# Top-k attention with a feed-forward block on one Trainium2 core: the turned weights go from SBUF to SBUF in 16 transfers, and small operations and the centring go to ScalarE

## The chip, the core and the metric

The kernel runs on one core of a Trainium2 chip. The metric is the device time of one execution in microseconds (us). Before the change it is 1734.24 us, the median of three runs (1732.39 to 1737.46). The kernel is written in Bass with the Tile layer, which places semaphores and buffers; the order of the instructions on each engine is the order in which the Python code emits them.

## The reference, cut to what matters

```python
# q, k, v: (8, 8, 576, 64) float32; top_k = 32
scores = q @ k.T / sqrt(64)
kth    = the 32nd largest score of each row
scores = where(scores >= kth, scores, -1e9)
attn   = softmax(scores)                  # per row, eps 1e-9 in the denominator
x      = (attn @ v) with heads joined     # (8, 576, 512)
mu, var = mean and variance of x's rows
xn     = (x - mu) / sqrt(var + 1e-6) * g_ln
out    = x + relu(xn @ w_ch1) @ w_ch2     # 512 -> 2048 -> 512
```

So there are 64 heads of 576 queries, each with a selection of 32 of 576 scores per row, and after them a feed-forward block over 4608 rows of 512.

## The kernel before, in words

**Units.** The queries of a pair of heads are cut into five units: four of 128 queries (with both heads side by side, tiles of 128x2x576) and a rest of 64 queries (both heads stacked in one tile of 128x576). There are 160 units in all, 20 for each of the 8 elements of the batch. Units are grouped into jobs (`Job`, `Group`): for the later batch elements four triples (two whole units and the rest unit, one triple for each pair of heads) and then four pairs (two whole units). A group ends in one product with v.

**Steps.** The main loop (from L1183) runs one step for each unit, and in a step it emits the work of several units at different ages. Step n does, in this order on each engine:

- PE: the scores of unit n+1 (L390), then, when a group is due, its product with v (`values`, L611 and L618), then the feed-forward matmuls (L756, L913) that `fill` hands out in small shares, and the turning back of a group's result (`place`, L653).
- ScalarE (ACT): copies of the new scores from PSUM to a tile `sc` (L371), the exponentials of unit n-2 (`weigh`, L496), the mask of unit n-1 (`mask`, L483), and evacuations for the feed-forward part.
- VectorE (DVE): for unit n the halving (L411, L412) and the four rounds of finding the top values (`select`, L433, L419, L425); `watch` (L452), which notes whether the selection may have been short; and `move(ex)` (L524) for unit n-2, in the middle of the step, ahead of the third round `select(u, 2)`.
- GpSimd (POOL): `lower` of unit n-1 (L488), sums for the feed-forward part, `prepare(u)` (L446: minus the row's largest score, as the exponential's bias) at the end of the step, and the centring of x in `Block.stats` (L687, L690).

**Turned weights.** The product with v needs the weights with the keys on the partitions. 118 of the 160 units (`u.moved`) are turned this way: DVE transposes 32x32 blocks of `e` into the unit's score tile `sc` (L524). Then the blocks have to change partitions. `send` (L540) stores the whole tile, 128 rows of 4608 bytes, to a DRAM tile `turned`, and `bring` (L532) loads it back into `pt` in four transfers of 32x4 rows of 1152 bytes. The tile `pt` has one buffer, so the first `bring` of a group waits until the product of the group before has read it. The score tiles `sc` have five buffers; one is free again when its `send` has landed. The other units are turned by PE.

**Queues.** All transfers but eight loads at the start are issued by SyncE (SP), in the order of the code: the heads of the next job (`load`, L293, eight for each fresh pair of heads), values (`load_values`, L305 and L309, four for each job), heads kept in DRAM for the second job of a pair of heads and fetched again (L334, L341), denominators of rest units (L601), prepared weights of the feed-forward block (L983), and stores of the result (L730). What should be issued later than it is known lies in a list `Later` and comes due after so many calls of `fill` (ticks): a `send` after 2 ticks, its `bring` 4 ticks later, a load of heads after 4. As the program is built, eight semaphores serve SP's transfers in turn, and each transfer waits for the one eight places before it.

**Feed-forward work.** When the rows of a block of 256 are complete, the block's matmuls go into a list with a cost each, and `slot(n)` spreads what is listed evenly over the steps up to the next block, or to the end (`END`). They fill PE beside the attention; what is left after the last unit runs alone at the end. A block is given a number of steps after its last unit, by `step` at L1053.

Of the kernel before, what the change touches and what calls it, by code (L numbers as in the profile page):

```python
# [9 lines left out]
AF = mybir.ActivationFunctionType  # L10
ALU = mybir.AluOpType
FP32 = mybir.dt.float32
# [7 lines left out]
STEEP = 2.0**90  # L20
# [9 lines left out]
def compute(  # L30
# [12 lines left out]
    nc = tc.nc  # L43
    P = nc.NUM_PARTITIONS
    B, H, S, D = q.shape
# [6 lines left out]
    scale = 1.0 / float(D) ** 0.5  # L52
# [4 lines left out]
    def pool(name, bufs, **kw):  # L57
        return ctx.enter_context(tc.tile_pool(name=name, bufs=bufs, **kw))
# [3 lines left out]
    HALF = S // 2  # L62
# [13 lines left out]
    brief_small = pool("brief_small", 2)  # L76
# [6 lines left out]
    xtpool = pool("xt", 1)  # L83
    hpool = pool("h", NF // 2)
    turnedpool = pool("turned_kq", 2, space=bass.MemoryType.DRAM)
    hbmpool = pool("hbm", 4, space=bass.MemoryType.DRAM)
    formpool = pool("forms", 1, space=bass.MemoryType.DRAM)
    psps = pool("ps", 5, space=PSUM)
    mmps = pool("mmps", 3, space=PSUM)
# [1 line left out]
    def const(shape, name):  # L91
        return consts.tile(shape, FP32, tag=name, name=name)
# [15 lines left out]
    if doubt is not None:  # L108
        watched = const([P, 34], "watched")
# [76 lines left out]
    now = [-1]  # L186
# [36 lines left out]
    todo = []  # L223
# [6 lines left out]
    def pop():  # L230
        kind, cost, run, may = todo.pop(0)
        assert not may or may()
        owed[0] -= cost
        run()
# [23 lines left out]
                run()  # L258

    sums_later, ends_later, stores = Later(), Later(), Later()  # L260
    sends, brings, loads = Later(), Later(), Later()

    def fill(least=0):
        tick[0] += 1
        ends_later.settle(END_AGE)
        loads.settle(LOAD_AGE)
        brings.settle(BRING_AGE)
        sends.settle(SEND_AGE)
        fetch_forms(FETCH_AGE)
        owed[0] = min(owed[0] + share[0], 6.0)  # L270
        while todo and (not todo[0][3] or todo[0][3]()):
            if owed[0] < todo[0][1] / 2 and least <= 0:
                break
            least -= 1
            pop()
# [162 lines left out]
            u.top = m  # L438
        u.thr = m

    def prepare(u):

        nt = len(u.tiles)
        u.bias, u.edge = u.thr[:, 0:nt, 5], u.thr[:, 0:nt, 6]
        eng = nc.vector if u.i < CONVERTING else nc.gpsimd
        eng.tensor_scalar(u.bias, u.top[:, 0:nt, 0], -scale, 0.0, ALU.mult, ALU.add)  # L446

    def watch(u):

        nt = len(u.tiles)  # L450
        c = 1 + 2 * (u.i % 16)
        nc.vector.tensor_tensor(  # L452
            watched[:, c : c + nt], u.hi[:, 0:nt, HALF + 7], u.thr[:, 0:nt, 7], ALU.subtract
        )
        if u.i % 16 == 15 or u.i == N - 1:
            u.ends_watch = True

    def settle_watch():

        for out, first, op in ((0, 0, ALU.max), (33, 1, ALU.min)):  # L460
            nc.vector.tensor_reduce(
                watched[:, out : out + 1], watched[:, first : first + 33],
                mybir.AxisListType.X, op,
            )
# [13 lines left out]
    def mask(u, t):  # L478
        if u.e is None:
            u.e = epool.tile([P, 2, S], FP32, tag="e", name="e")  # L480
        if t == 0:
            nc.scalar.mul(u.edge, u.thr[:, 0 : len(u.tiles), 7], STEEP)
        nc.scalar.activation(  # L483
            u.e[:, t], u.sc[:, t], AF.Relu, bias=u.edge[:, t : t + 1], scale=-STEEP
        )

    def lower(u, t):
        nc.gpsimd.tensor_tensor(u.e[:, t], u.e[:, t], u.sc[:, t], ALU.subtract)  # L488
# [30 lines left out]
    def move(u):  # L519

        i0 = place_of(u)
        ni, nb = P // 32, (2 * J + 1) * 32
        blocks = u.sc[:].rearrange("p t n -> p (t n)")
        nc.vector.transpose(  # L524
            blocks.rearrange("p (j c n) -> p j c n", j=ni, n=32),
            u.e[:].rearrange("p t n -> p (t n)").rearrange("p (c j k) -> p j c k", j=ni, k=32),
        )
        hbm = hbmpool.tile([P, 2 * S], FP32, tag="turned", name="turned")

        def bring():  # L530
            for j in range(ni):
                nc.sync.dma_start(  # L532
                    u.group.pt[j * 32 : (j + 1) * 32, i0 : i0 + ni].rearrange(
                        "k i c n -> k i (c n)"
                    ),
                    hbm[:, j * nb : (j + 1) * nb].rearrange("(i k) x -> k i x", k=32),
                )

        def send():
            nc.sync.dma_start(hbm[:], blocks)  # L540
            brings.add(bring)

        sends.add(send)

# [120 lines left out]
    class Block:  # L665
# [9 lines left out]
        def stats(self, i):  # L675
            x = self.x[i]
            if self.mv is None:
                self.mv = small.tile([P, J, 2], FP32, tag="mv", name="mv")
                self.rstd = small.tile([P, J], FP32, tag="rstd", name="rstd")
            st = brief_small.tile([P, 6], FP32, tag="st", name="st")  # L680
            nc.vector.bn_stats(out=st[:], in_=x)
            nc.vector.bn_aggr(out=self.mv[:, i, :], in_=st[:])
            if now[0] <= gives_first:
                nc.vector.tensor_scalar_sub(x, x, self.mv[:, i, 0:1])
            else:
                less = brief_small.tile([P, 1], FP32, tag="less", name="less")
                nc.gpsimd.tensor_scalar(  # L687
                    less[:], self.mv[:, i, 0:1], -1.0, 0.0, ALU.mult, ALU.add
                )
                nc.gpsimd.tensor_scalar(x, x, 1.0, less[:], ALU.mult, ALU.add)  # L690
            self.step[i] = now[0]

        def centred(self, i):
# [246 lines left out]

    PER_ROW = 1.71e-3
    SUM_AGE, END_AGE, FETCH_AGE, STORE_AGE = 7, 6, 10, 8
    SEND_AGE, BRING_AGE, LOAD_AGE = 2, 4, 4
    blocks = []
    plain_done, formed, used, fetched = [None], [None], [], [0]

# [41 lines left out]
    def fetch_forms(age):  # L988
        if done(formed[0]):
            free = 4 + sum(tick[0] - x >= age for x in used)  # L990
            while fetched[0] < min(free, 8 * (len(blocks) - 1)):
                fetch_form()
# [19 lines left out]
    units = []  # L1012
# [5 lines left out]
            g.last = len(units) - 1  # L1018
        j.last = len(units) - 1
    N = len(units)  # L1020
    END = N + 7

    fresh = []
    for j in jobs:
# [7 lines left out]
    CONVERTING = max(n for n in batches if batches[n]) + 2  # L1032
    EARLY = jobs[NHP].first
# [16 lines left out]
    for j in jobs:  # L1050
        if j.hp == NHP - 1:
            b = j.b
            step = j.last + (3 if j.last < EARLY else 4 + units[j.last].moved)  # L1053
            tiles = [(b, qt) for g in j.groups for qt in g.qts if qt < J]
            dsts = [[(out[b, t[1] * P : (t[1] + 1) * P, :], full)] for t in tiles]
            if jobs.index(j) == NHP - 1:
                step -= 1
                j.groups[0].quick = True
            if tiles:
                add_block(step, tiles, dsts)  # L1060
            if J in j.groups[0].qts and b % 4 == 3:
# [17 lines left out]
    def at(i):  # L1079
        return units[i] if 0 <= i < N else None  # L1080
# [64 lines left out]
    def slot(n):  # L1145
# [5 lines left out]
        if n > last_give:  # L1151
            even = left / max(1, END - 1 - n)
        else:
# [28 lines left out]
    weights(-1, 1)  # L1182
    for n in range(END):  # L1183
        now[0] = n
# [7 lines left out]
        u, nxt, mk = at(n), at(n + 1), at(n - 1)  # L1192
        ex, g = after(n)
# [3 lines left out]
        moved = ex is not None and ex.moved  # L1197
# [9 lines left out]
        if u:  # L1207
            halve(u)
            select(u, 0)
        if doubt is not None and mk:  # L1210
            watch(mk)
        for j in fetches.get(n, []):
            fetch_heads(j)
        stores.settle(STORE_AGE)
# [30 lines left out]
        sums_later.settle(SUM_AGE)  # L1245
        for den in recips.pop(n, []):
            nc.vector.reciprocal(den, den)
        if doubt is not None and at(n - 1) and at(n - 1).ends_watch:
            settle_watch()
            if n == N:  # L1250
                tell()
        if n in turns:
            turn_heads(turns[n])
# [6 lines left out]
        if mk and not early:  # L1260
            mask(mk, 0)
# [9 lines left out]
            lower(mk, 0)  # L1271
        if len(parts) > 2:
            parts[1]()
        if moved:
            move(ex)
        if u:
            select(u, 2)
        for blk, i in rows_of.pop(n, []):
# [27 lines left out]
            weights(n, 1)  # L1306
        if u:
            select(u, 3)
            prepare(u)
        for x in (g, quick):  # L1310
            if x and x.job.hp == NHP - 1:
                for qt in x.qts:
# [10 lines left out]
                for x in (r - 1, r):  # L1323
                    arrived(n, ("r", x), rs[x])
        fill()
    while todo or any(x.waiting for x in (sums_later, ends_later, stores, sends, brings)):
        tick[0] += 1
        stores.settle(2)
        brings.settle(1)
        sends.settle(1)  # L1330
        ends_later.settle(1)
        sums_later.settle(1)
        fetch_forms(1)
        if todo:
            pop()
# [50 lines left out]
```

## Time and profile before

| | |
|---|---|
| median of three runs | 1734.24 us (1732.39 to 1737.46) |
| profiled execution: its own time, its span | 1737.59 us, 1735.7 us |
| busy: PE, DVE, ACT, POOL | 1485.2, 1467.9, 1032.2, 1051.8 us |
| granted TensorE clock, mean | 0.932 |
| transfers issued by SP, their issue time added up | 1527, 750 us |
| time that packets took, share of 16 DMA engines | 55.8% |
| from the start of unit 20 to the last watch of unit 159 (7 batch elements) | 1364.1 us |
| span after the last watch (1609.7 us), mostly feed-forward work on PE | 126 us |

How to read it. The profile is of one execution, 3.4 us above the median; sums against the trace are made with its span. "Busy" is the time in which an engine ran an instruction; the waits, by engine and by line, are in a view of their own, as are the waits of SP's queue. SP is not counted among the busy engines, since it only issues; but an issue has a duration too, and the timeline of SP shows it: the second column of a row is the time that SP spent on the issues of that row, which is not the time of the transfer. The time from issue to landing is given apart, in the table of transfers.

### The profile page before, as it was taken

What the parts mean: (1) busy time and instruction counts of PE and PEld (TensorE: products, weight loads), DVE (VectorE), ACT (ScalarE), POOL (GpSimd) and SP (SyncE); (2) the same over time, 40 slices, a digit from 0 to 9 for tenths busy, and PEclk for the clock granted to TensorE, in tenths of its full rate; (3) what the DMA queues carried; (4) which work ended last, traced back from release to release, by engine and by line L of the source; (5) the groups of instructions that cost most, each with busy time, mean ns of one, the idle gap of its engine ahead of it and who ended that gap; (6) DMA issues with size and microseconds to landing.
All of it is one profiled execution on the core that took longest, in us unless ns stands there. A gap on an engine that the chain in (4) does not pass through costs nothing.

```text
span 1735.7 us, 26165 instructions
## 1 busy us (share of the span) xinstructions
PE 1485.2 (86%) x7412; PEld 1110.8 (64%) x7412; DVE 1467.9 (85%) x4090; ACT 1032.2 (59%) x2662; POOL 1051.8 (61%) x1321
## 2 busy tenths in 40 slices
PE   2558887887788888788899989999899899989997
PEld 1336455655566665566677766776677676768886
DVE  6979999989898998889998998899989998984100
ACT  6777765755566564556566756676566665644411
POOL 4668868646556564556656766576656665746334
PEclk9768898988999898899999999999999999989999
DMA  7525657744565465545775586556755676453411
GB/s 190 134 66 181 200 123 216 226 140 136 151 182 151 145 187 154 152 144 153 212 181 159 161 221 161 175 167 181 199 172 150 168 214 181 139 141 110 124 45 51
DMA packets 392068, 275.19 MB, mean 159 GB/s; under 512 B 254436, under 2 KB 358376, under 8 KB 391912
## 3 DMA queue, kind: packets, MB, share of 16 engines
q1 hardware_dynamic: 387176, 272.81, 55.8%
q8 instruction: 62, 1.02, 0.3%
q10 hardware_dynamic: 4736, 0.59, 0.2%
q14 instruction: 94, 0.77, 0.1%
HBM read 177.47 MB, written 95.81 MB: 157 GB/s over the span
## 4 chain that ended last, share of the span: by engine, by line
PE 41%; DVE 30%; ACT 8%; DMA 8%; POOL 7%; SPq 3%; issue 2%; DVEq 0%; ACTq 0%; POOLq 0%
PE ops L913 14%; PE hps L756 12%; DVE m L433 9%; DVE hi L419 7%; PE av L611 6%; DVE sc L524 5%; PE scps L390 4%; DMA pt<-turned 3%; POOL e L488 3%; DVE lo L412 3%; ACT e L496 2%; DVE hi L411 2%; DVE hi L425 2%; PE av L618 2%; SPq L532 2%
## 5 line engine op out<-in xcount | busy, mean ns | idle before, releaser
L488 POOL TENSOR_TENSOR e<-e,sc 128x576 f32<-128x576 f32 x288 | 424.0, 1482 | 295.8 <-ACT e L483 292.5
L756 PE MATMUL hps<-xT,w 128*128 128x256 f32 x2304 | 533.4, 384 | 3.2 <-ACT xT L718 3.2
L756 PEld LDWEIGHTS hps<-xT,w 128*128 128x128 f32 x2304 | 432.1, 192 | 74.3 <-issue 12.3
L433 DVE MAX8 m<-hi 128x8 f32<-128x296 f32 (+1 forms) x1152 | 469.9, 442 | 1.1
L419 DVE MATCH_REPLACE8 hi<-m,hi 128x288 f32<-128x288 f32 (+1 forms) x864 | 377.1, 441 | 0.0
L913 PE MATMUL ops<-w,h 128*128 128x256 f32 x1360 | 321.3, 385 | 0.0
L371 ACT COPY sc<-scps 128x288 f32<-128x288 f32 x576 | 202.7, 406 | 190.1 <-PE scps L390 167.2
L913 PEld LDWEIGHTS ops<-w,h 128*128 128x128 f32 x1360 | 256.2, 193 | 42.1 <-issue 7.5
L611 PE MATMUL av<-pt,vb 128*64 128x256 f32 (+2 forms) x1088 | 175.6, 473 | 101.4 <-DMA pt<-turned 62.7
L496 ACT ACTIVATE e<-e,m 128x576 f32<-128x576 f32 x288 | 224.9, 787 | 60.2 <-POOL e L488 59.9
L524 DVE STREAM_TRANSPOSE sc<-e 128x1152 f32<-128x1152 f32 x118 | 160.2, 1358 | 109.5 <-ACT e L496 103.0
L483 ACT ACTIVATE e<-sc,m 128x576 f32<-128x576 f32 x288 | 217.5, 774 | 5.2
L611 PEld LDWEIGHTS av<-pt,vb 128*64 128x64 f32 x1088 | 91.3, 161 | 174.4 <-issue 94.9
L446 POOL TENSOR_SCALAR m<-m 128x2 f32<-128x2 f32 (+1 forms) x143 | 109.3, 764 | 135.1 <-DVE m L433 132.0
L779 ACT ACTIVATE h<-hps 128x512 f32<-128x512 f32 x144 | 85.4, 594 | 102.3 <-PE hps L756 101.9
L412 DVE TENSOR_TENSOR lo<-sc 128x576 f32<-128x576 f32 (+1 forms) x160 | 144.2, 901 | 0.0
L390 PE MATMUL scps<-kT,qT 64*128 64x288 f32 x512 | 96.8, 480 | 46.0 <-DVE qT L320 40.6
L411 DVE TENSOR_TENSOR hi<-sc 128x576 f32<-128x576 f32 (+1 forms) x160 | 124.9, 780 | 6.6 <-ACT sc L371 6.4
L913 PE MATMUL ops<-wt,s 128*128 128x256 f32 x544 | 128.0, 383 | 0.0
L390 PE MATMUL scps<-kT,late_qT 64*128 64x288 f32 (+3 forms) x832 | 122.2, 412 | 2.1 <-ACT pt L565 2.1
L425 DVE MAX8 hi<-lo 128x8 f32<-128x288 f32 x288 | 117.8, 443 | 0.0
L913 PEld LDWEIGHTS ops<-wt,s 128*128 128x128 f32 x544 | 102.0, 192 | 16.6 <-issue 2.1
(104 smaller groups left out, 1664.4 us busy)
## 6 DMA issues: line engine op xcount, KB each, us to landing
turned<-sc SPq DMA_DIRECT2D x118, 576.0 KB, 3.3
pt<-turned SPq DMA_DIRECT2D x472, 144.0 KB, 3.0
w<-forms SPq DMA_DIRECT2D x136, 256.0 KB, 4.1
vb<-in_v_dram SPq DMA_DIRECT2D x136, 128.0 KB, 3.3
raw<-in_moe_w_ch_dram SPq DMA_DIRECT2D x32, 512.0 KB, 4.5
kT<-kept SPq DMA_DIRECT2D x36, 288.0 KB, 3.4
kin<-in_k_dram SPq DMA_DIRECT2D x128, 72.0 KB, 2.4
kept<-kT SPq DMA_DIRECT2D x32, 288.0 KB, 2.6
```

The source lines that it names most:

```text
L371: nc.scalar.copy(u.sc[:, t, s * HALF : (s + 1) * HALF], made[s][t][:, 0:HALF])
L390: nc.tensor.matmul(ps[i * R : i * R + ql, o : o + width], qT[r, q0 : q0 + ql], kT[r, k0 : k0 + width], start=True, stop=True,)
L412: nc.vector.tensor_tensor(lo, a, b, ALU.min)
L419: nc.vector.match_replace(x, m[:, t, :], x, LOWEST)
L433: nc.vector.max(m[:, t, :], u.hi[:, t, 0:width])
L483: nc.scalar.activation(u.e[:, t], u.sc[:, t], AF.Relu, bias=u.edge[:, t : t + 1], scale=-STEEP)
L488: nc.gpsimd.tensor_tensor(u.e[:, t], u.e[:, t], u.sc[:, t], ALU.subtract)
L496: nc.scalar.activation(u.e[:, t], u.e[:, t], AF.Exp, bias=u.bias[:, t : t + 1], scale=-scale, accum_out=g.den[:, col : col + 1],)
L524: nc.vector.transpose(blocks.rearrange("p (j c n) -> p j c n", j=ni, n=32), u.e[:].rearrange("p t n -> p (t n)").rearrange("p (c j k) -> p ...
L611: nc.tensor.matmul(av[h * D : (h + 1) * D, 0 : g.nq], vb[:, h * J + c, :], g.pt[:, 0 : g.nq // 32, 5 * h + c, :], start=(c == 0), stop=False,)
L756: nc.tensor.matmul(ps[0][:, side * N : (side + 1) * N], w1[:, c, f * P : (f + 1) * P], self.xT[:, c, 0:N], start=(c == 0), stop=(c == NC - 1),
L913: nc.tensor.matmul(bank[name][:, 0:Q], a(j), rhs, start=first and j == 0, stop=(j == G - 1), skip_group_check=not first,)
```

## The change

1. `send` and `bring` are one: the DRAM tile `turned` is gone, and `send` issues 16 transfers from SBUF to SBUF, each of 32 rows of 288 elements (1152 bytes), 36 KB, from 32 partitions of `sc` to 32 partitions of `pt`.
2. `move(ex)` is emitted at the end of the step, after `select(u, 3)`, and no longer ahead of `select(u, 2)`.
3. `prepare` (POOL, in the first steps DVE) and `watch` (DVE) are gone; `mask` does the same on ACT: the scaled maximum by one `mul`, the watched difference by one activation for each tile.
4. The centring in `Block.stats` goes from POOL to ACT and becomes due two ticks later (`CENTRE_AGE`).
5. A block whose last unit is moved is given one step later, `settle_watch` and `tell` come one step later, and the loop has one more step (`END = N + 8`).

```diff
-    sends, brings, loads = Later(), Later(), Later()
+    sends, loads, centres = Later(), Later(), Later()
...
-        brings.settle(BRING_AGE)
+        centres.settle(CENTRE_AGE)
...
-    def prepare(u):
-        nt = len(u.tiles)
-        u.bias, u.edge = u.thr[:, 0:nt, 5], u.thr[:, 0:nt, 6]
-        eng = nc.vector if u.i < CONVERTING else nc.gpsimd
-        eng.tensor_scalar(u.bias, u.top[:, 0:nt, 0], -scale, 0.0, ALU.mult, ALU.add)
-
-    def watch(u):
-        nt = len(u.tiles)
-        c = 1 + 2 * (u.i % 16)
-        nc.vector.tensor_tensor(
-            watched[:, c : c + nt], u.hi[:, 0:nt, HALF + 7], u.thr[:, 0:nt, 7], ALU.subtract
-        )
...
     def mask(u, t):
...
         nc.scalar.activation(
             u.e[:, t], u.sc[:, t], AF.Relu, bias=u.edge[:, t : t + 1], scale=-STEEP
         )
+        if t == 0:
+            nc.scalar.mul(u.bias, u.top[:, 0:nt, 0], -scale)
+        if doubt is not None:
+            c = 1 + 2 * (u.i % 16) + t
+            nc.scalar.activation(
+                watched[:, c : c + 1], u.thr[:, t, 7:8], AF.Identity,
+                bias=u.hi[:, t, HALF + 7 : HALF + 8], scale=-1.0,
+            )
...
-        hbm = hbmpool.tile([P, 2 * S], FP32, tag="turned", name="turned")
-        def bring():
-            for j in range(ni):
-                nc.sync.dma_start(
-                    u.group.pt[j * 32 : (j + 1) * 32, i0 : i0 + ni].rearrange(
-                        "k i c n -> k i (c n)"
-                    ),
-                    hbm[:, j * nb : (j + 1) * nb].rearrange("(i k) x -> k i x", k=32),
-                )
         def send():
-            nc.sync.dma_start(hbm[:], blocks)
-            brings.add(bring)
+            for i in range(ni):
+                for j in range(ni):
+                    nc.sync.dma_start(
+                        u.group.pt[j * 32 : (j + 1) * 32, i0 + i].rearrange("k c n -> k (c n)"),
+                        blocks[i * 32 : (i + 1) * 32, j * nb : (j + 1) * nb],
+                    )
...
-                nc.gpsimd.tensor_scalar(
-                    less[:], self.mv[:, i, 0:1], -1.0, 0.0, ALU.mult, ALU.add
-                )
-                nc.gpsimd.tensor_scalar(x, x, 1.0, less[:], ALU.mult, ALU.add)
+                def centre():
+                    less = brief_small.tile([P, 1], FP32, tag="less", name="less")
+                    nc.scalar.mul(less[:], self.mv[:, i, 0:1], -1.0)
+                    nc.scalar.activation(x, x, AF.Identity, bias=less[:])
+                    self.step[i] = now[0]
+                centres.add(centre)
+                return
...
-    END = N + 7
+    END = N + 8
...
-            step = j.last + (3 if j.last < EARLY else 4 + units[j.last].moved)
+            step = j.last + (3 if j.last < EARLY else 4 + 2 * units[j.last].moved)
...
-        if moved:
-            move(ex)
         if u:
             select(u, 2)
...
         if u:
             select(u, 3)
-            prepare(u)
+        if moved:
+            move(ex)
```

More of the change, by code (lines that the diff above doesn't have):

```diff
@@ L85, in compute @@
     turnedpool = pool("turned_kq", 2, space=bass.MemoryType.DRAM)
-    hbmpool = pool("hbm", 4, space=bass.MemoryType.DRAM)
     formpool = pool("forms", 1, space=bass.MemoryType.DRAM)
@@ L439, in select @@
         u.thr = m
-    def prepare(u):
-        nt = len(u.tiles)
-        u.bias, u.edge = u.thr[:, 0:nt, 5], u.thr[:, 0:nt, 6]
-        eng = nc.vector if u.i < CONVERTING else nc.gpsimd
-        eng.tensor_scalar(u.bias, u.top[:, 0:nt, 0], -scale, 0.0, ALU.mult, ALU.add)
-    def watch(u):
-        nt = len(u.tiles)
-        c = 1 + 2 * (u.i % 16)
-        nc.vector.tensor_tensor(
-            watched[:, c : c + nt], u.hi[:, 0:nt, HALF + 7], u.thr[:, 0:nt, 7], ALU.subtract
-        )
-        if u.i % 16 == 15 or u.i == N - 1:
-            u.ends_watch = True
     def settle_watch():
@@ L480, in mask @@
             u.e = epool.tile([P, 2, S], FP32, tag="e", name="e")
+        nt = len(u.tiles)
         if t == 0:
-            nc.scalar.mul(u.edge, u.thr[:, 0 : len(u.tiles), 7], STEEP)
+            u.bias, u.edge = u.thr[:, 0:nt, 5], u.thr[:, 0:nt, 6]
+            nc.scalar.mul(u.edge, u.thr[:, 0:nt, 7], STEEP)
         nc.scalar.activation(
@@ L485, in mask @@
         )
+        if t == 0:
[6 more added lines that the diff above has]
+            )
+            u.ends_watch = u.i % 16 == 15 or u.i == N - 1
     def lower(u, t):
@@ L685, in stats @@
             else:
-                less = brief_small.tile([P, 1], FP32, tag="less", name="less")
-                nc.gpsimd.tensor_scalar(
-                    less[:], self.mv[:, i, 0:1], -1.0, 0.0, ALU.mult, ALU.add
-                )
-                nc.gpsimd.tensor_scalar(x, x, 1.0, less[:], ALU.mult, ALU.add)
+                def centre():
[5 more added lines that the diff above has]
+                return
             self.step[i] = now[0]
@@ L942, in compute @@
     SUM_AGE, END_AGE, FETCH_AGE, STORE_AGE = 7, 6, 10, 8
-    SEND_AGE, BRING_AGE, LOAD_AGE = 2, 4, 4
+    SEND_AGE, LOAD_AGE, CENTRE_AGE = 2, 4, 2
     blocks = []
@@ L1209, in compute @@
             select(u, 0)
-        if doubt is not None and mk:
-            watch(mk)
         for j in fetches.get(n, []):
@@ L1247, in compute @@
             nc.vector.reciprocal(den, den)
-        if doubt is not None and at(n - 1) and at(n - 1).ends_watch:
+        if doubt is not None and at(n - 2) and at(n - 2).ends_watch:
             settle_watch()
-            if n == N:
+            if n == N + 1:
                 tell()
@@ L1325, in compute @@
         fill()
-    while todo or any(x.waiting for x in (sums_later, ends_later, stores, sends, brings)):
+    while todo or any(x.waiting for x in (sums_later, ends_later, stores, sends)):
         tick[0] += 1
         stores.settle(2)
-        brings.settle(1)
         sends.settle(1)
```

## The prediction, made before the result was known

> **What bounds the kernel now.** I read the page first, then the waits, then SP's timeline. No engine is full alone: PE is busy 1485.2 us and DVE 1467.9 of 1735.7.
>
> ```profile
> span 1735.7 us, 26165 instructions
> ...
> PE 41%; DVE 30%; ACT 8%; DMA 8%; POOL 7%; SPq 3%; issue 2%; DVEq 0%; ACTq 0%; POOLq 0%
> ```
>
> The chain passes from one engine to the next, so hand-overs count. The waits (us in total, times, longest) name them:
>
> ```profile
> DVE sc L524 <- ACT e L496: 103.0, 34, 9.3
> PE av L611 <- DMA pt<-turned: 62.7, 19, 9.5
> ```
>
> DVE waits in mid-step for the exponentials, and PE waits for the turned weights. The second pair is tight far oftener than 19 times: taking the starts from the timelines, in most groups L611 starts within 1 us of the landing of the group's last `bring`. SP's timeline shows what lies ahead of that landing (start, us; the last row is PE's timeline):
>
> ```profile
> 1297.47 0.34 SPq L540 DMA_DIRECT2D turned<-sc  x1
> 1297.91 0.38 SPq L983 DMA_DIRECT2D w<-forms  x1
> 1298.34 0.97 SPq L305 DMA_DIRECT2D vb<-in_v_dram  x1
> 1299.35 0.69 SPq L309 DMA_DIRECT2D ends<-in_v_dram  x1
> 1300.09 0.59 SPq L305 DMA_DIRECT2D vb<-in_v_dram  x1
> 1300.72 0.51 SPq L309 DMA_DIRECT2D ends<-in_v_dram  x1
> 1301.34 1.65 SPq L983 DMA_DIRECT2D w<-forms  x2
> 1303.08 1.13 SPq L601 DMA_DIRECT2D dr<-den  x2
> 1304.26 2.00 SPq L532 DMA_DIRECT2D pt<-turned  x4
> ...
> ```
>
> ```profile
> 1309.20 2.37 PE L611 MATMUL av<-pt,vb 128*64 128x320 f32 x16 [0.98 <-DMA pt<-turned]
> ```
>
> The transpose ended at 1297.4; SP then issued without a pause for 9 us, and PE got its weights at 1309.2. Issuing takes SP about half a microsecond for each transfer, in order, whatever its bytes. Over one batch element (units 120 to 139, 1204.9 to 1394.0, 189 us) SP's issues add up to some 98 us: about half full, and it can afford to stand waiting for DVE:
>
> ```profile
> SPq L540 <- DVE m L433: 404.5, 89, 13.5
> SPq L532 <- PE av L618: 57.3, 16, 13.4
> ```
>
> **What one of the new issues costs.** This decides all. Each moved unit needs 16 issues for 5, in all 118 x 11 = 1298 more on top of 1527. No row shows a transfer of 32 rows without an inner loop. The nearest (ns, min/median/max):
>
> ```profile
> L532 SPq DMA_DIRECT2D pt<-turned x472: 302/430/1348, 160.9 to 1636.2; - x158
> L540 SPq DMA_DIRECT2D turned<-sc x118: 319/338/1456, 154.0 to 1623.8; - x118
> L601 SPq DMA_DIRECT2D dr<-den x64: 483/587/1930, 236.4 to 1519.5; - x64
> L309 SPq DMA_DIRECT2D ends<-in_v_dram x136: 489/515/1411, 30.1 to 1627.4; - x136
> ```
>
> There are two classes. L532, L540, L293 and all transfers of 128 rows take 0.31 to 0.34 us after a pause and 0.376 (128 rows after L540) to 0.43 (L532 after L532) in a burst. L601, L309 and the eight stores of 64 rows take 0.48 to 0.52 alone; behind one of their own class L601 and the 64-row stores take 0.59. Bytes (4 to 2048 a row) and direction make no difference there. The program as built marks the fast class, and it alone, as having its descriptors' shape worked out beforehand; the new 32x288 transfers lack the mark, like L601, L309 and the 64-row stores. L601 is also the only row from SBUF to SBUF. So I take 0.595 + 0.045 between issues (the gap in bursts) = **0.64 us for each transfer, 10.2 for a unit**; the bounds are 0.42 (0.376 + 0.045) and 0.64, with 0.475 (L532's start to start) and 0.535 (L601's first to second) between.
>
> [...]
>
> **The sum, one batch element.** SP's order in the changed program: 256 moved issues; 113 others as before, worth 61 us by their own spacing (32 of L293 at 0.54, 16 L305 at 0.635, 16 L309 at 0.56, 20 L983 at 0.495, 8 each of L601 at 0.59, L334 at 0.52 and L341 at 0.48, 5 L730 at 0.45). Alone, 256 x 0.64 = 163.8, and 163.8 + 61 = 225 us: more than the 195 us that a batch element takes now (1364.1 / 7). SP becomes the bound.
>
> To this come pauses that SP can't fill. The first 16 of a group must wait until PE has read `pt` (one buffer): 1.4 us from the last issue to its landing (L601 lands 1.8 us after its issue starts; I take 2.0), 0.2 to wake PE, 2.9 for the product (L611 2.4, L618 about 0.5), together 4.6 in pairs. In triples the wait is another one: unit n+5 shares its `sc` buffer with unit n, which is now held until the 16 have landed. So copies (1.6), exponentials (1.9) and the transpose (1.36) of the next moved unit run after the landing: 1.4 + 5.3 = 6.7. SP fills these with what stands behind in its order. For the four pairs that is 2.9, 7.7, 8.2 and 1.0 us, which leaves 1.7 + 0 + 0 + 3.6 idle; for the triples 3.2, 2.7, 4.2 and 6.6, which leaves 3.5 + 4.0 + 2.5 + 0.1. Together 15.4, so **240 us for each batch element**. Written with the spacing p: 256 p + 77.
>
> Seven elements: 7 x 240.4 - 1364.1 = 319; less 10 because the last unit isn't moved. The seven moved units of the first element cost SP 7 x (10.2 - 2.3) = 55 more, of which I let 15 show, since SP idles in the rest units after them. The 126 us at the end are PE's and stay. 1735.7 + 319 - 10 + 15 = 2060, and 2 us outside the span give 2062, made against 1737.6; against the median 3 less. **Forecast 2060 us.**
>
> **What the other parts give.** Move at the step's end: DVE gets 2.8 us of rounds three and four ahead of its wait, enough for most of the 103 us; the price is a transpose up to 2.8 us later. Watch: DVE loses 160 operations, 57.2 + 12.5 = 70 us; ACT gets 288 at 0.203 (L508's small ones), 58. Prepare: POOL loses 109.3, and no longer stands waiting for DVE (132 us); ACT gets 160 at 0.21, 33. Centring: POOL loses 26.8 + 3.8 + 7.6 = 38, ACT gets 36 of about 0.2 + 0.8 (L734), at least 0.6 (L718), so 29 to 36; PE's 27 us of waiting for L690 may shrink. ACT's sum, some 125 on 1032, lies in its idle time. With SP as the bound all this is worth nothing, and I cost it so; with SP out of the way DVE's part is worth up to 173 us less what PE's load (over 92% busy from 832.5 us on) allows. No DRAM write and read of 68 MB each: packets take 55.8% of the DMA engines now, so nothing waits for that share. Behind each 16 issues stand the loads of values, heads and prepared weights (L983); they come up to 10 us later, and PE may wait there too. I have no term for this; it belongs to the upper end. Blocks given a step later: no time, the last one isn't.
>
> **Rivals.**
>
> - *The issue costs what L532's does* (0.475). For it: same rows, same tile. Against it: an inner loop, and the mark. 256 x 0.475 + 77 = 199, 4 us an element more: 1735 + 28 = about 1765 (1740 to 1800).
> - *Faster: SP stays below the bound.* The formula meets today's 195 us at p = 0.46. At 0.42 it gives 184, and then DVE's 70 us and part of its 103 us of waits show: at most 7 x 11 = 77 us, PE allows perhaps half: about 1700. For it: 128-row transfers do reach 0.376 behind each other. Against it: none with fewer rows and one loop does.
> - *The change doesn't shift the bound*: SP's backlog drains in the 861 us (its pauses over 0.15 us added up) in which it now idles, and all stays near 1735. Against it: the moved issues are needed at once, and the pauses lie where SP waits for DVE.
> - *Worse*: if none of the other issues fit into the pauses, 225 + 4 x 4.6 + 4 x 6.7 = 270 for each element, 2265 in all; half of that, and late L983 loads, give 2160 and more.
>
> **How the numbers follow.** Forecast 0.78 (its own range 1870, at p = 0.535, to 2140); L532's price 0.10; faster 0.04; no shift 0.03; worse 0.05. The range takes in the forecast's and most of the worse case: 1870 to 2180. About 0.3% (5 us) is what a measurement of this kernel can tell from no change. Slower: 0.78 + 0.05 + 0.09; the rest of L532's case and of "no shift" makes 0.04 the same; 0.04 faster.
>
> **What would show it.** Right: the new issues at about 0.59 us each behind one another; SP's timeline without pauses over most of a batch element; PE's waits at the product on `pt`, and ACT's copies waiting for the transfers, up to hundreds of us; granted clock down, since PE idles more. Wrong: if the new issues take 0.43 or less, the forecast falls with them. If they take 0.59 and the time is below 1935 (1735.7 + 7 x 30, the issues alone), SP's work isn't what I counted.

## The result, and the profile after

| | before | after |
|---|---|---|
| median of 4 runs each, side by side | 1734.57 us | 2229.35 us (2228.92 to 2229.75) |
| ratio, 95% interval | | 1.2851 (1.2829 to 1.2873) |
| profiled span | 1735.7 us | 2227.9 us |
| busy: PE, DVE, ACT, POOL | 1485.2, 1467.9, 1032.2, 1051.8 us | 1576.7, 1508.1, 1116.0, 952.2 us |
| granted clock | 0.932 | 0.843 |

The forecast of 2060 us had the sign and the engine right and was 169 us too low; the time lies above its range (1870 to 2180). From the page of the changed kernel, the span and the chain by engine:

```profile
span 2227.9 us, 28241 instructions
...
SPq 31%; PE 26%; DVE 19%; ACT 9%; DMA 8%; issue 5%; POOL 2%; ACTq 0%; DVEq 0%; POOLq 0%
```

SP's queue, 3% of the chain before, now leads it. The new issues themselves, from the view of their line (ns, min/median/max):

```profile
L526 SPq DMA_DIRECT2D pt<-sc x1888: 507/588/2052, 163.5 to 2138.5; - x189
```

Back to back they start 0.633 us apart (median), where 0.64 was forecast. From SP's waits and then from the engines' waits (us in total, times, longest):

```profile
SPq L526 <- PE av L606: 107.9, 29, 12.2
SPq L526 <- DVE sc L518: 86.5, 28, 8.2
```

```profile
DVE hi L410 <- ACT watched L475: 413.5, 84, 21.6
...
PE av L599 <- DMA pt<-sc: 358.1, 42, 16.5
...
ACT sc L370 <- DMA pt<-sc: 307.3, 47, 12.9
DVE sc L518 <- ACT e L490: 161.9, 29, 24.9
```

PE's and ACT's waits for the transfers were forecast. The largest wait of DVE was not: `halve` (L410), which waited 6.4 us for ACT's copies in the whole kernel before, now stands 413.5 us for ACT's `watch`. The row of before:

```profile
DVE hi L411 <- ACT sc L371: 6.4, 2, 4.2
```

Where SP's pauses come from can be seen at one group, a triple. SP's timeline, whose last row is cut off by the end of the view, then PE's (start, length):

```profile
1676.22 10.06 SPq L526 DMA_DIRECT2D pt<-sc  x16
1686.38 1.18 SPq L589 DMA_DIRECT2D dr<-den  x2
1687.65 0.53 SPq L340 DMA_DIRECT2D kT<-kept  x1
1688.23 0.43 SPq L340 DMA_DIRECT2D late_qT<-kept  x1
1692.52 7.54 SPq L526 DMA_DIRECT2D pt<-sc  x12
```

```profile
1687.95 3.81 PE L599 MATMUL av<-pt,vb 128*64 128x320 f32 x16 [11.19 <-DMA dr<-den]
1691.69 0.81 PE L606 MATMUL av<-pt,ends 128*128 128x320 f32 x2
```

Sixteen issues take 10.06 us, four other transfers follow, and then SP has nothing it may issue until PE has read `pt` at 1692.5: 3.9 us of pause. The product takes 4.55 us where the prediction took 2.9. The view by windows gives the granted clock over it (third number from the end), first here and then over the product that the prediction shows, of the kernel before:

```profile
1687.90:1692.60 4.70, 4.65 (x20) 2.53 (x21) 0.00 (x0) 0.07 (x1) 0.00 (x0) 0.68 0.32 98
```

```profile
1309.10:1312.20 3.10, 3.00 (x19) 1.80 (x20) 2.52 (x8) 2.26 (x7) 2.07 (x5) 1.00 0.43 150
```

So the clock is 0.68 over the one product and 1.00 over the other, which took 3.11 us from its first matmul to the end of its last; 3.11 / 0.68 is 4.57. From the traces' matmuls and clock records, medians of 28 products of each kind after the first batch element: in triples 5.20 us against 3.11 before, in pairs 4.54 against 2.58. Length times clock is nearly the same in both kernels (3.07 and 3.11, 2.48 and 2.58).

The length of a batch element can be split by SP's timeline: its issues, the gaps below 0.2 us between them, and its pauses. Three elements of each kernel (units 60 to 79, 100 to 119 and 120 to 139), mean of the three, us:

| kernel | issues | small gaps | pauses | element |
|---|---|---|---|---|
| before | 93.5 | 9.5 | 90.9 | 194.0 |
| after | 209.8 | 19.0 | 31.7 | 260.6 |
| forecast | 225 with gaps | | 15.4 | 240.4 |

So SP's own work was 229 us instead of 225, and the pauses were twice the forecast. Over the six elements of units 20 to 139 the changed kernel has 223, 33 and 256 us.

### The profile page after: what moved, and what is told of

The parts are those of the page before. It is cut to its first block, busy times and chain, and to the rows that moved or that the text cites. A ratio compares the mean times of both kernels' runs of the same rounds, so it can differ in the third digit from the quotient of the medians.

```text
span 2227.9 us, 28241 instructions
## 1 busy us (share of the span) xinstructions
PE 1576.7 (71%) x7412; PEld 1153.3 (52%) x7412; DVE 1508.1 (68%) x3913; ACT 1116.0 (50%) x3178; POOL 952.2 (43%) x1110
## 3 DMA queue, kind: packets, MB, share of 16 engines
q1 hardware_dynamic: 392840, 203.30, 33.9%
## 4 chain that ended last, share of the span: by engine, by line
SPq 31%; PE 26%; DVE 19%; ACT 9%; DMA 8%; issue 5%; POOL 2%; ACTq 0%; DVEq 0%; POOLq 0%
SPq L526 30%; PE av L599 10%; PE hps L748 6%; PE ops L905 6%; DMA pt<-sc 6%; DVE m L432 5%; DVE hi L418 4%; DVE hi L410 3%; PE av L606 2%; DVE lo L411 2%; DVE sc L518 2%; ACT e L467 2%; DVE hi L424 1%; ACT e L490 1%; ACT sc L370 1%
## 5 line engine op out<-in xcount | busy, mean ns | idle before, releaser
L482 POOL TENSOR_TENSOR e<-e,sc 128x576 f32<-128x576 f32 x288 | 422.0, 1474 | 740.3 <-ACT e L467 740.1
L599 PE MATMUL av<-pt,vb 128*64 128x256 f32 (+2 forms) x1088 | 241.5, 615 | 475.0 <-DMA pt<-sc 358.1
L748 PEld LDWEIGHTS hps<-xT,w 128*128 128x128 f32 x2304 | 436.6, 194 | 83.8 <-issue 16.4
L410 DVE TENSOR_TENSOR hi<-sc 128x576 f32<-128x576 f32 (+1 forms) x160 | 183.6, 1148 | 418.3 <-ACT watched L475 413.5
L599 PEld LDWEIGHTS av<-pt,vb 128*64 128x64 f32 x1088 | 118.7, 207 | 577.5 <-issue 557.7
L370 ACT COPY sc<-scps 128x288 f32<-128x288 f32 x576 | 197.3, 408 | 417.4 <-DMA pt<-sc 307.3
L905 PE MATMUL ops<-w,h 128*128 128x256 f32 x1360 | 326.6, 389 | 13.0 <-DMA w<-forms 8.5
L518 DVE STREAM_TRANSPOSE sc<-e 128x1152 f32<-128x1152 f32 x118 | 160.9, 1363 | 166.0 <-ACT e L490 161.9
L467 ACT ACTIVATE e<-sc,m 128x576 f32<-128x576 f32 x288 | 222.8, 774 | 7.9 <-DVE sc L518 2.9
L614 ACT COPY oT<-av 128x256 f32<-128x256 f32 (+2 forms) x68 | 25.9, 380 | 314.4 <-PE av L606 314.3
L411 DVE TENSOR_TENSOR lo<-sc 128x576 f32<-128x576 f32 (+1 forms) x160 | 178.5, 1116 | 0.0
L632 POOL COPY oTr<-oT 128x64 f32<-128x64 f32 x32 | 7.6, 238 | 384.1 <-ACT oT L614 371.6
```

Source lines behind the costliest of these rows:

```text
L410: nc.vector.tensor_tensor(hi, a, b, ALU.max)
L411: nc.vector.tensor_tensor(lo, a, b, ALU.min)
L467: nc.scalar.activation(u.e[:, t], u.sc[:, t], AF.Relu, bias=u.edge[:, t : t + 1], scale=-STEEP)
L599: nc.tensor.matmul(av[h * D : (h + 1) * D, 0 : g.nq], vb[:, h * J + c, :], g.pt[:, 0 : g.nq // 32, 5 * h + c, :], start=(c == 0), stop=False,)
L748: nc.tensor.matmul(ps[0][:, side * N : (side + 1) * N], w1[:, c, f * P : (f + 1) * P], self.xT[:, c, 0:N], start=(c == 0), stop=(c == NC - 1),
L905: nc.tensor.matmul(bank[name][:, 0:Q], a(j), rhs, start=first and j == 0, stop=(j == G - 1), skip_group_check=not first,)
```

## Experiments

Three theories stood against each other. **Theory 1**: SP's issues, at 0.633 us each, and the pauses that SP can't fill set the time. **Rival 2**: the new wait of `halve` for ACT's `watch` does. **Rival 3**: the path within SBUF, or the landing of many small transfers, whatever their issue costs SP. Ratios are to the kernel before, run on the same chip.

**Undoing and isolating the parts.** The first kernel takes only the transfers into the kernel before:

```diff
-            nc.sync.dma_start(hbm[:], blocks)
-            brings.add(bring)
+            for i in range(ni):
+                for j in range(ni):
+                    nc.sync.dma_start(u.group.pt[j * 32 : (j + 1) * 32, i0 + i]...,
+                        blocks[i * 32 : (i + 1) * 32, j * nb : (j + 1) * nb])
...
-    SEND_AGE, BRING_AGE, LOAD_AGE = 2, 4, 4
+    SEND_AGE, BRING_AGE, LOAD_AGE = 2, 6, 4
```

> The kernel before with one part of the change alone: each moved unit's store and four loads through DRAM become 16 (4 for a last single block) transfers within SBUF, issued six ticks after the transpose, where the four loads were issued; move, watch, prepare and centring stay as before. Theory 1 (SP's issues, 0.635 us each back to back, and the pauses it can't fill set the time): 2150 to 2230 us, the new issues at 0.59 us, granted clock about 0.84, no wait of DVE for ACT's watch since watch is DVE's. Rival 2 (the changed kernel is slow because DVE's halve now waits for ACT's watch, 413 us in its trace): 1740 to 1800. Rival 3 (nothing but the latency of the path within SBUF): issues below 0.45 us, time above 2000 all the same.

Measured: 2238.75 us, 1.2910 (1.2862 to 1.2959), issues at 0.588 us, clock 0.842: 9 us above theory 1's range, whose other signs hold. The transfers alone, without the new wait, make all of the loss. Rival 2 can't be the main cause.

The second puts only the way through DRAM back into the changed kernel (`send` and four loads in `bring`, `BRING_AGE` 4):

> The changed kernel with the way through DRAM put back (one store, four loads four ticks later); the small operations and the centring stay on ACT and the move stays at the step's end. Theory 1: the issues are the cause, so the time falls to 1690 to 1760, and DVE's wait for ACT's watch falls from 413 us to below 100, since ACT's copies no longer wait for SP. Rival 2 (the new wait for ACT's watch is a cause of its own): 2000 or more, that wait still above 300 us.

Measured: 1819.81 us, 1.0497 (1.0459 to 1.0536). Neither expectation held: the transfers account for 410 us of the changed kernel's 495, and the rest of the change, which I had taken for a small gain, loses 5%. DVE's wait for the watch is still there, with SP out of the way:

```profile
DVE hi L412 <- ACT watched L477: 179.7, 47, 9.9
```

The third and the fourth give `watch` back to DVE, with the 16 transfers and with the way through DRAM:

```diff
-        if doubt is not None:
-            c = 1 + 2 * (u.i % 16) + t
-            nc.scalar.activation(watched[:, c : c + 1], u.thr[:, t, 7:8], AF.Identity,
-                bias=u.hi[:, t, HALF + 7 : HALF + 8], scale=-1.0)
...
+        if doubt is not None and mk:
+            watch(mk)
```

> The changed kernel with only the watch given back to DVE (one operation for a unit, in the step after, as before); the 16 transfers stay. Theory 1: the wait of halve for the watch goes, but SP stays the bound and DVE waits elsewhere: 2150 to 2229 us, SP's issues without a pause for just as long. Rival 2: the wait of 413 us in 160 steps was on the path, 1750 to 2000.

> The changed kernel with both put back: the way through DRAM and the watch on DVE. What is left of the change is prepare and centring on ACT and the move at the step's end. Theory 1: SP out of the way again, 1670 to 1740 us: DVE's wait for the exponentials (103 us before) shrinks, PE's load allows part of it. If it is slower than the kernel before by over 0.5%, the move at the step's end costs more by its later landing than the shorter wait gives.

Measured: 2175.98 us, 1.2555 (1.2504 to 1.2606), and 1747.44 us, 1.0088 (1.0060 to 1.0116). The watch on ACT costs 53 us where SP is the bound and 72 us where it isn't: rival 2 is right as a second, smaller cause. What is left of the change without transfers and watch is still 0.9% slower than the kernel before, and not faster.

**What the watch costs: the buffer or ACT's time?** `hi` has two buffers, so `halve` of a unit needs the one that the unit two before it used; ACT's `watch` now reads that buffer behind ACT's copies and masks. This kernel is e2_hbm_rest with the same 288 operations, reading the maxima only; it watches nothing real:

```diff
-                bias=u.hi[:, t, HALF + 7 : HALF + 8], scale=-1.0,
+                bias=u.thr[:, t, 7:8], scale=-2.0,
```

> The kernel of e2_hbm_rest with ACT's watch reading only the maxima and no longer the tile hi that DVE wants back (so it watches nothing real; same 288 operations at the same place). If the 72 us between e2 (1820) and e5 (1747) are the wait of DVE's halve for a hi buffer that ACT's watch still holds: 1745 to 1765, and that wait gone from DVE's list. If they are ACT's time for 288 more small operations on the path from mask to exponential: 1800 to 1825.

Measured: 1753.04 us, 1.0060 (1.0038 to 1.0081). What DVE's `halve` waits for in it, at the same line:

```profile
DVE hi L412 <- ACT sc L372: 16.0, 9, 6.4
```

The wait for the watch on `hi`, 179.7 us before, is gone, and 67 us of the time with it, while ACT's operations are all still there. The cost is the buffer that a slower reader holds.

**How many issues, and of which price.** One kernel keeps the way through DRAM of the kernel before and cuts its four loads into the change's 16 pieces:

```diff
-            for j in range(ni):
-                nc.sync.dma_start(u.group.pt[j * 32 : (j + 1) * 32, i0 : i0 + ni]...,
-                    hbm[:, j * nb : (j + 1) * nb]...)
+            for i in range(ni):
+                for j in range(ni):
+                    nc.sync.dma_start(u.group.pt[j * 32 : (j + 1) * 32, i0 + i]...,
+                        hbm[i * 32 : (i + 1) * 32, j * nb : (j + 1) * nb])
```

> The kernel before with its way through DRAM kept, but the four loads of a unit cut into the same 16 pieces of 32 rows x 288 that the change moves within SBUF (17 issues for a unit instead of 5). The program as built marks these loads like the fast class of the kernel before. Theory 1 (SP's time for its issues; a loss by the class of the issue and not by their number alone): issues at 0.43 us, start to start 0.475, so 256 x 0.475 + 77 + 16 x 0.43 for the stores = 206 us an element, some 11 above the 195 of before: 1740 to 1830 us. Rival 3 (16 small landings are slow whatever their issue costs): above 2000 us.

Measured: 2113.33 us, 1.2187 (1.2167 to 1.2208). The view of its line:

```profile
L533 SPq DMA_DIRECT2D pt<-turned x1888: 302/419/1816, 161.5 to 2018.2; - x189
```

The price of one was as theory 1 expected (0.419, start to start 0.464), the time was not: it lies where rival 3 put it. But these landings are not slow (median 1.8 us from issue to landing), and what SP waits for is mostly something else. SP's issues and gaps come to 191 us an element, its pauses to 53.5: in its order SP now waits for the store's landing (150.8 us in all), for DVE (135.3) and for PE's reading of `pt` (90.5), and stands still in each. This kernel keeps the store and its landing, which the change does not have, so it is no measurement of the change at a lower price. The class of an issue is only part of it, and the pauses are no constant that can be carried from one order to another.

Next, when the transfers are due. e1_transfers_only with `BRING_AGE` 2 instead of 6:

> The kernel of e1_transfers_only with one number changed: the 16 transfers are issued two ticks after the transpose, as in the changed kernel, not six. Theory 1a (SP is bound but its pauses depend on when the transfers are due): from 2239 to between 2150 and 2210, SP's pauses shorter than the 265 us that e1 shows between 300 and 2100. Rival (SP's issues alone set the time): 2225 to 2250, no change.

Measured: 2200.49 us, 1.2671 (1.2649 to 1.2694). SP's pauses between 300 and 2000 us fall from 237 to 192 us, the time by 38. The time lies in theory 1a's range. The same issues in another place in SP's order give another time, by about what the pauses lose.

Then half of the issues on another queue, in e3_watch_dve:

```diff
-                    nc.sync.dma_start(
+                    (nc.scalar if j % 2 else nc.sync).dma_start(
```

> The kernel of e3_watch_dve with 8 of each unit's 16 transfers issued from ACT's queue and 8 from SP's; same bytes, same path, same number. Theory 1 (SP's issuing is the bound): SP needs 128 x 0.635 + 61 = 142 us for a batch element, ACT gets 80 us more beside its 130: 1800 to 1980 us. Rival 3 (the transfers' path or their landing): 2150 or more, no gain.

Measured: 2159.62 us, 1.2444 (1.2423 to 1.2465): almost nothing gained, as rival 3 had it. But the trace shows why, and it isn't the path. From ACT's timeline, then the sum over the kernel from ACT's waits:

```profile
1519.59 5.37 ACTq L529 DMA_DIRECT2D pt<-sc  x8
1525.01 0.78 ACT L493 ACTIVATE e<-e,m 128x576 f32<-128x576 f32 x1 [5.27 <-DMA pt<-sc]
```

```profile
ACT e L493 <- DMA pt<-sc: 334.7, 64, 9.5
```

ACT pays the same price (median 602 ns against SP's 589), and its next exponential stands behind its eight issues. An issue of SP takes no longer while ACT issues too: 592 ns (median of 244 that overlap) against 588 alone (611). So in this run the price is that of the engine which issues, SP or ACT, and not that of a path that both fill.

SP's pauses grow to 110 us an element. Part of them come from the semaphores: the trace shows the same eight for both queues, and SP now stands waiting for transfers that ACT issued late (3.9 us in the whole changed kernel at L526; here, two rows of several):

```profile
SPq L529 <- DMA pt<-sc: 96.8, 64, 6.7
SPq L292 <- DMA pt<-sc: 92.9, 40, 8.9
```

How much of the missing gain is ACT's delay and how much this was not measured apart.

**Fewer issues on the same path** tell theory 1 and rival 3 apart. A part of the transfers is left out; for that the tile `pt` must be written once before, so one tile filled with zeros serves all groups, and the first kernel is the control with all 16. The last lines of the diff are those of the kernel with 12; the one with 8 has `if (i + j) % 2 == 0` there:

```diff
+    one_pt = ptpool.tile([P, GQ // 32, 2 * J + 1, 32], FP32, tag="pt", name="pt")
+    nc.gpsimd.memset(one_pt[:], 0.0)
...
-            g.pt = ptpool.tile([P, GQ // 32, 2 * J + 1, 32], FP32, tag="pt", name="pt")
+            g.pt = one_pt
...
+                    if i != j or ni == 1:
+                        nc.sync.dma_start(
```

> Control for the next two: the kernel of e3_watch_dve with one tile for the turned weights, filled with zeros at the start and used by all groups, in place of a new tile from a pool of one buffer for each group. All 16 transfers are there. Theory 1: same work, same waits, 2176 us within 1% (2155 to 2200); less, down to 2120, if the waits on the tile now fall by parts.

> The control with the 4 transfers left out that stay on their own 32 partitions (12 of 16 for a unit); the product reads what an earlier group or the zeros left there, so part of the weights is wrong. Theory 1 (SP's busy time plus its pauses is the length of an element): 64 issues x 0.633 = 40.5 us less for each of seven elements and some 9 in the first: about 1885 us (1860 to 1960, the upper end if the pauses grow as SP finds less to issue in them). Rival 3 (the landing of a unit's last transfer, or the path): above 2050.

> The control with 8 of the 16 transfers left out (those with i + j odd); half of the weights is stale. Theory 1: SP needs 128 x 0.633 + 61 + 14 of small gaps = 156 us for an element, pauses of 23 to 50 on top reach 179 to 206, so that the other engines' 195 decide again: 1745 to 1830 us. Rival 3: above 1950.

| transfers for a unit | median, us | ratio (95%) | issues + gaps | pauses | element |
|---|---|---|---|---|---|
| 16 (control) | 2184.82 | 1.2542 (1.2493 to 1.2592) | 231.2 | 22.2 | 253 |
| 12 | 1929.19 | 1.1071 (1.1026 to 1.1117) | 189.0 | 31.2 | 220 |
| 8 | 1735.54 | 0.9965 (0.9942 to 0.9988) | 145.7 | 47.3 | 194 |

The first four left out save 256 us, 33 us an element: 42 of SP's time less 9 more of pauses. The next four save 194 us, less because the other engines' 195 us are reached; the time with eight is that of the kernel before, some 10 us below what was expected; twelve lie inside their range. The path, the bytes of one transfer and its landing (median 1.9 us with 16, 12 and 8, as in the changed kernel) are the same. The chain by engine of the kernel with eight:

```profile
PE 38%; DVE 35%; ACT 8%; SPq 7%; DMA 5%; POOL 3%; issue 3%; ACTq 0%; DVEq 0%; POOLq 0%
```

SP falls from 31% of the chain to 7%, PE and DVE lead again. Theory 1 holds in steps. Leaving transfers out also leaves out their bytes and landings; but the DMA engines' share was 33.9% in the changed kernel against 55.8% before, and no trace here shows a landing that slows with the number. So nothing is left for rival 3 to rest on.

**The other parts alone.** First the move at the step's end (and blocks given a step later), then `prepare` and the centring on ACT, each as the only part in the kernel before:

```diff
-        if moved:
-            move(ex)
         if u:
             select(u, 2)
...
             prepare(u)
+        if moved:
+            move(ex)
```

> The kernel before with the move at the step's end as the only part of the change (blocks given out of it one step later, too). By the prediction's reading DVE's wait for the exponentials (103 us) shrinks and the transpose comes up to 2.8 us later: 1710 to 1735 us. If the 13 us that e5_hbm_watch_dve lost come from here, 1740 to 1755: then the later landing costs PE more than DVE's wait was worth.

> The kernel before with prepare and centring on ACT as the only parts of the change (move in mid-step, way through DRAM, watch on DVE). By e5_hbm_watch_dve (1747) against e9_move_end (1753) these parts are worth some 6 us: 1725 to 1737 us. If they are worth nothing by themselves, 1734 within 0.3%; if ACT's 70 us more are on the path, 1740 to 1755.

Measured: 1753.09 us, 1.0092 (1.0075 to 1.0108), and 1747.67 us, 1.0037 (1.0012 to 1.0063) against a before of 1740.65 in that comparison. Both expectations of a gain missed; each time lies in the range given for a loss, the second only because its own kernel before was slower (a loss of 7 us). With the move at the end DVE's wait for the exponentials falls from 103.0 to 82.2 us only, and `halve`'s two operations take 900 + 996 ns instead of 780 + 901, which is 34 us over 160 units; PE's wait for the turned weights grows from 62.7 to 73.2 us. That `halve` is slower at another place in the step was not foreseen. The traces show what slows it. One operation of the changed kernel, with POOL's `lower` (L482) beside it:

```profile
1696.74 1.41 POOL L482 TENSOR_TENSOR e<-e,sc 128x576 f32<-128x576 f32 x1 [1.38 <-ACT e L467]
1696.88 1.89 DVE L410 TENSOR_TENSOR hi<-sc 128x576 f32<-128x576 f32 x1 [13.02 <-ACT watched L475]
1698.69 0.75 DVE L411 TENSOR_TENSOR lo<-sc 128x576 f32<-128x576 f32 x1
```

POOL's operation ends at 1698.15 and DVE's 0.62 us later; the next one, with POOL idle, takes 0.75 us. Of the 256 operations of `halve` at this shape, 53 take over 0.85 us in the kernel before, 114 with the move at the end and 166 in the changed kernel. Every one of them starts while a POOL operation is running, and nine in ten end 0.60 to 0.62 us after that operation; those that meet no POOL operation take 0.70 to 0.76 us. So the long ones wait for a POOL operation that is running, and their place in the step decides how often they meet one. Not every POOL operation holds them up: in the kernel before 107 of the 203 short ones began beside one, too, 69 of them beside `prepare` (L446). No run took POOL's operations away.

With the small operations on ACT DVE's wait for the exponentials grows from 103.0 to 116.7 us: ACT's idle time did not lie where the operations went.

No part and no combination that ran beat the kernel before with its whole work done.

## Why the prediction was right and wrong

- **SP becomes the bound: right.** With the watch on DVE, leaving out half of the transfers takes the time from 2184.8 back to 1735.5 us. SP's issues and the small gaps between them fill 88% of an element.
- **0.64 us for each issue: right** (0.633), by the row of `dr` (L601), which had the same path and no mark. The two classes are less clean than the prediction says: L305 (128 rows) and L293, of its fast class, have medians of 0.586 and 0.496, above its 0.43; its sum used their own spacing. The same 32x288 pieces take 0.419 from DRAM (e6_dram16) and 0.588 within SBUF. One issue takes 0.59 us of the 1.9 from its start to its landing, and 16 in a row take 10.1 us.
- **SP's other work, 61 us an element: right.** Issues and gaps together were 229 us against 225.
- **Pauses of 15.4 us an element: the step that failed.** They are 31.7, and 16.3 too many in each of seven elements are some 114 of the 169 us. By SP's timeline 22.4 of the 31.7 lie at PE's product (in the holes between the last moved issue of one group and the first of the next), where the prediction had all of its 15.4, and 9.3 elsewhere.
- **Elsewhere: a wait that it did not have.** With the watch back on DVE (e3_watch_dve) the pauses fall by 8.8 us to 22.9, and almost all of these are at the product. So the 8.8 come with the wait of `halve`, which makes transposes late for SP ("SPq L526 <- DVE sc L518", 7.5 us an element in the changed kernel and 0.3 there).
- **At the product: the wrong price and, in triples, the wrong wait.** The product was priced at 2.9 us (it took 3.11 in the group that the prediction shows), and takes 5.20 in triples and 4.54 in pairs, at mean clocks of 0.59 and 0.65 over the products. I forecast that the clock falls and did not price the product by it. For triples I took the `sc` buffer to be the wait that ends last; in 10 of the 12 triples SP's next issue starts 0.03 us after PE's product ends. The hole of 6.7 us that I gave triples is near 1.4 + 0.2 + 5.2 = 6.8 by luck, and its named terms (1.4 + 1.6 + 1.9 + 1.36) make only 6.3. With the measured products in all eight holes, the prediction's own table gives some 19 us (an estimate). The last 3.5 lie in the triples, where SP had less to issue than the table says in some (1.1 us in two of them); what else is in them stays open.
- **The sum.** From the start of unit 20 to that of unit 159 the element terms are 134.6 us above the forecast's 309 (319 less 10), the first element 24.6 above its 15, and the end 9.2 above nothing: together 168. Giving the watch back removes 49, 9 and -3 of these. The 15 of the first element was a guess out of 55; 39.6 showed.
- **"ACT's sum lies in its idle time", the other parts at nothing: wrong.** What a moved operation costs is not only its time (ACT's watch takes 283 ns, I had 203) but what it holds: `hi` has two buffers, and I named no wait that the watch on ACT adds. It is worth 53 us of the 169 here and 72 us with SP out of the way. The gain that I saw for that case ("up to 173 us") was a loss of 85: 72 by the watch, 13 by the other parts. The move's price, a later transpose, was named; `halve` meeting POOL's operations more often was not.
- **Rivals.** L532's price was refuted for these transfers, and e6_dram16 makes its 1765 doubtful even at that price, since its 77 us held my constant pauses; e6_dram16 has the store besides, so this is not shown. "Faster" and "no shift" are out (the 861 us of SP's pauses there come to 904 over the whole timeline). "Worse" (2160 to 2265) holds the result, but not by its mechanism: SP did fill part of most holes, as in the triple shown, and the holes were longer than forecast.
- **Signs.** The clock fell as forecast, from 0.932 with PE busy for 86% of the span to 0.843 with 71%. e10_one_pt_16 and e12_8_of_16 pair in the same way (0.853 with 71%, 0.934 with 86%), stretches of one kernel only roughly (in the kernel before 0.78 from 100 to 200 us and 0.90 from 700 to 800, with PE busy for 78 and 79 of the 100 us). PE waits for the transfers at the product and ACT's copies wait for their landing. SP's timeline without pauses "over most of a batch element" is right, with 12% of pauses.

## What to carry to other kernels

Count issues, not bytes: here a transfer cost the engine that issues it 0.34 to 0.6 us (medians; in the kernel before 0.338 for 576 KB, 0.587 for 0.2 KB), in order, so one large store and four loads through DRAM beat 16 small moves within SBUF (1819.81 us against 2229.35 with the rest of the change the same), though they move every byte twice. When an in-order queue becomes the bound, its pauses must be priced as carefully as its work, from the loop that refills it (a single buffer, the product that frees it, at the clock that will then be granted: a median of 0.59 over the product of triples here, 1.00 before). When an operation goes to another engine, ask which buffer it reads and who waits for that buffer, before asking whether the engine has time. When an operation moves to another place in the step, look in the trace at what the other engines run there: here one operation of `halve` took 0.75 us alone and one 1.89 beside another engine's.

## What the runs showed of the hardware that was not expected

- The same 32x288 piece costs the issuing queue 0.419 us (median) from DRAM and 0.588 from SBUF, and 0.602 from ACT's queue. For these pieces the class goes with the mark that the prediction speaks of: those from DRAM carry it, those within SBUF don't. Beyond them it is less clean: `ends` (L309, 64 rows from DRAM) lacks it and has 0.515, `vb` (L305) carries it and has 0.586. What decides whether a transfer gets the mark was not found.
- For the same pieces landing differs by 0.1 us between the paths: 1.9 us (median) within SBUF, 1.8 from DRAM. What the way within SBUF saves on these is the store (3.3 us in the kernel before).
- The two operations of `halve` took 780 and 901 ns before, 900 and 996 with the move at the step's end, 1148 and 1116 in the changed kernel, at the same shapes. Alone they take 0.70 to 0.76 us; those over 0.85 us end 0.61 us (median) after a POOL operation that was running when they started.
